# A product that scales w2 moves from POOL to DVE, two tiles change places, and six late sums change engine

## Chip, cores and metric

The kernel runs on one core of one Trainium2 chip. The metric is the time of one execution on the device in microseconds; the kernel before has a median of 1222.18 us over three runs (1219.56 to 1225.83). A core has five engines, each with its own queue of instructions that it works off in order: PE multiplies matrices, DVE, ACT and POOL work elementwise, and SP issues the transfers. They wait for one another through semaphores.

## The reference

A transformer block on 2048 tokens of width D = 576, all in float32, with six vectors of length 576 that are computed from a condition vector `c`:

```python
mod = (_silu(c) @ w_mod).reshape(c.shape[0], 6, 1, -1)
sa, ca, ga, sb, cb, gb = (mod[:, 0], mod[:, 1], mod[:, 2], mod[:, 3], mod[:, 4], mod[:, 5])
h = _layernorm(x, axis=-1) * (1 + ca) + sa
x = x + ga * _A_ref(h, A_wqkv, A_wo)        # linear attention, 32 heads
h = _layernorm(x, axis=-1) * (1 + cb) + sb
x = x + gb * _B_ref(h, B_w1, B_w2)          # silu(h @ w1) @ w2, F = 4608
```

The change concerns the last line, the feed-forward part. Its output is scaled by `gb`, one factor for each output column; the kernel multiplies the columns of w2 by `gb` instead.

## The kernel before

**Three stages.** Up to about 250 us the kernel computes the attention's projections, and up to about 398 us the attention's output, the second layer norm and the first 256 of the 4608 hidden columns. From there to the end it works on the other 17 groups of 256 hidden columns, numbered 1 to 17 (`NG` is 18). This third stage is where the diff lies.

**The third stage.** The tokens are four blocks of 512, taken as two pairs. A unit (class `Unit`) is one group of hidden columns with one pair of blocks. Both multiplications of a unit, up (by w1, `up`, L960) and down (by w2, `down`, L1048), are done in the Strassen-Winograd way: seven products of half-sized matrices in place of eight, for sums and differences of the quarters. Every operand is split into a rounded part, which ACT writes as a cast, and the rest, which DVE or POOL writes as a difference (`sub_hi` at L62, `split` at L1008 and L1009), so that each product takes three passes. The operands of `up` from the tokens have been stored in DRAM (`hd`) and are streamed through three buffers called rooms; each pass that ends starts the next fetch (L936).

**The weights of a group** (class `Weights`). `load1` brings a group's part of w1 into the tile `raw` (L890, and two transfers of 64 rows, L892), `sums1` makes four sums on POOL (L881 to L884) in the temporary tile `t`, and `up(n)` splits operand n into one of eight tiles `w1` (cast L902, difference L62). `load2` brings the group's part of w2 into the same tile `raw` (L908); `sums2` multiplies it by gb (L912, on POOL, 128 partitions of 2 x 576 values), makes four more sums on POOL, and `down` splits the results (cast L924, difference L62). The tile `wt` holds the last 64 rows of w1. `raw`, `t` and the `w1` tiles lie in one pool of SBUF memory, `wm`, with `raw` first; one `raw` exists at a time.

**What a unit computes.** The products of `up` are put together by DVE from PSUM (L977, L984, L998) into tiles `f`, and ACT applies SiLU (L980, L999). `operands1` and `operands2` make the operands of `down`: `ha` and `hb` are split on DVE, `hd`, `hc` and `he` on POOL, which also makes the sums before them (L1018, L1024, L1026, L1029). The products of `down` are added by DVE from PSUM into the output in SBUF, `acc`, or into one tile `U` for each block (L1052).

**U.** One of Winograd's sums is common to three quarters of the output. It is collected in `U` over all groups, and in the last group `add_u` (L1066) adds it to the three quarters of each block, after which the quarters are stored (L1071). For blocks 0, 1 and 3 these sums are on POOL, for block 2 on DVE. Block 3's own last group is computed without Winograd (`plain_operands`, `plain_down`, L1085 to L1089), so its `U` is complete one unit earlier; the program adds it after the last unit's loop.

**Order.** PE's instructions are in the order of the program: in each unit, the seven products of `up` in turn, and between them the fourteen products of `down` of the unit before. The other engines' instructions are ordered by a scheduler that simulates the program, with the program's order as the priority, so an edit in one place can move instructions on DVE, ACT, POOL and SP around it. Two PSUM tiles hold the results of `down`: a product that begins a new sum in one of them waits until DVE has added the old one (L1052), and the second product of a pair in one tile waits until DVE has read the first.

Of the kernel before, what the change touches and what calls it, by code (L numbers as in the profile page):

```python
# [9 lines left out]
F32R = mybir.dt.float32r  # L10
# [5 lines left out]
P = 128  # L16
# [5 lines left out]
def kernel(ctx: ExitStack, tc, A_x, A_wqkv, A_wo, B_x, B_w1, B_w2, c, w_mod, out):  # L22
# [8 lines left out]
    V, A, G, T = nc.vector, nc.scalar, nc.gpsimd, nc.tensor  # L31
# [3 lines left out]
    S, D = x.shape  # L35
# [11 lines left out]
    G2 = 2  # L47
# [13 lines left out]
    def sub_hi(lo, full, hi):  # L61
        return V.tensor_sub(lo, full, f32(hi))  # L62
# [4 lines left out]
    accp = tc.alloc_tile_pool(name="acc", bufs=1)  # L67
    hTa = tc.alloc_tile_pool(name="hTa", bufs=2)
    wg = tc.alloc_tile_pool(name="wg", bufs=2)
    wp = tc.alloc_tile_pool(name="w", bufs=3)  # L70
    wqp = tc.alloc_tile_pool(name="wq", bufs=1, side="right")
# [9 lines left out]
    bc = {n: pool.tile([P, D], F32, name=f"bc_{n}") for n, pool in (("ga", pa), ("gb", const))}  # L81
# [334 lines left out]
    for t in range(NT):  # L416
        tb, i = t // 4, t % 4
# [28 lines left out]
        for _ in range((0, 2, 1, 1)[t] if t < 4 else 1):  # L446
            q = next(qs)
# [42 lines left out]
    for j, kv in enumerate(kvp):  # L490
        n = min(2, NHC - 2 * j)
# [90 lines left out]
    def load_mlp(g):  # L582
        f0 = g * FW
        r1 = rawp.tile([P, KC + 1, FW], F32, name="raw")
        nc.sync.dma_start(r1[:, 0:KC, :], B_w1[0 : KC * P, f0 : f0 + FW].rearrange("(k p) f -> p k f", p=P))
        for h in range(2):
            nc.sync.dma_start(r1[h * 64 : h * 64 + 64, KC, :], B_w1[KC * P : D, f0 : f0 + FW])
        w1 = wg.tile([P, 9, FW], F32R, name="w")
        A.copy(w1[:, 0:KC, :], r1[:, 0:KC, :])
        sub_hi(w1[:, KC : 2 * KC, :], r1[:, 0:KC, :], w1[:, 0:KC, :])  # L590
        wt = rawp.tile([P, 2, FW], F32R, name="wt")
        G.memset(f32(wt[64:128, 1, :]), 0.0)
        tail_w(wt, r1[:, KC, :])
        r2 = rawp.tile([P, KC + 1, FW], F32, name="raw").rearrange("p k f -> p (k f)")[:, : G2 * D]
        r2 = r2.rearrange("p (j d) -> p j d", j=G2)
        nc.sync.dma_start(r2, B_w2[f0 : f0 + FW, :].rearrange("(j p) d -> p j d", p=P))
        w2 = wg.tile([P, G2, 2, D], F32R, name="w")
        V.tensor_mul(r2, r2, bc["gb"].unsqueeze(1).to_broadcast([P, G2, D]))
        A.copy(w2[:, :, 0, :], r2)
        sub_hi(w2[:, :, 1, :], r2, w2[:, :, 0, :])  # L600
        return w1, w2, wt
# [57 lines left out]
    def mlp_units(tb, w):  # L659

        hs = new_hs()
        up = [lambda j=j: mlp_up(tb, w[0], w[2], hs, j) for j in range(G2)]
        return up, [lambda i=i: mlp_down(4 * tb + i, hs, w[1]) for i in range(4)]
# [38 lines left out]
    def turn_all(tb):  # L702
# [16 lines left out]
        else:  # L719
# [29 lines left out]
            else:  # L749
# [3 lines left out]
                for k in CHUNKS:  # L753
                    turn_chunk_k(tb, k, rows[:, k] if k < KC else t)
                    yield
        up, down = mlp_units(tb, w)
        if tb < NB - 1:
            filler.extend(up + down)
# [39 lines left out]
    while s < NT + 5 or filler or turns:  # L798
        if s < QB - 2:
            filler.append(late_q)  # L800
        if s == 4:
            w = load_mlp(0)
# [36 lines left out]
    psC = tc.alloc_tile_pool(name="psC", bufs=1, space=PSUM, reuse_waits="tile")  # L839

    w2p = tc.alloc_tile_pool(name="w2p", bufs=1, reuse_waits="tile")
    wm = tc.alloc_tile_pool(name="wm", bufs=1, reuse_waits="tile")
    pf = tc.alloc_tile_pool(name="pf", bufs=1, reuse_waits="tile")
    first = tc.alloc_tile_pool(name="first", bufs=1, reuse_waits="tile")
    rs = tc.alloc_tile_pool(name="rs", bufs=1, side="right", reuse_waits="tile")
# [4 lines left out]
    U = [pf.tile([P, 2, HALF], F32, name=f"U{b}") for b in range(NB)]  # L850
# [14 lines left out]
    class Weights:  # L865
# [32 lines left out]
            tail_w(self.wt, self.r1[:, KC, :])  # L898

        def up(self, n):  # L900
            w = self.w1[n] = wm.tile([P, 4, P], F32R, name="w1", bufs=8)
            A.copy(w[:, 0:2], self.b1[n])  # L902
            sub_hi(w[:, 2:4], self.b1[n], w[:, 0:2])

# [4 lines left out]

        def sums2(self):  # L910
            r2, t = self.r2, self.temps(HALF)
            G.tensor_mul(r2, r2, bc["gb"].unsqueeze(1).to_broadcast([P, G2, D]))  # L912
            parts = [r2[:, j, k * HALF : (k + 1) * HALF] for j in range(2) for k in range(2)]
            if self.last:
                self.split2("B12", parts[1])
            self.b2 = self.winograd(*parts, [t[:, i] for i in range(3)])
# [14 lines left out]
    def fetch(i):  # L931
        if i < len(streamed):
            _, q, n = streamed[i]
            room = rooms0[ORDER[i]] if i < 3 else rooms[i % 3]
            m = hd[q, n].shape[1]
            nc.sync.dma_start(f32(room[:, :m, :]), hd[q, n])  # L936
            in_room[i] = room

    class Unit:
# [123 lines left out]

        def add_u(self, b, *parts):
            for i, k in parts:
                (V if self.pair == 1 and b == 2 else G).tensor_add(self.c(b, i, k), self.c(b, i, k), U[b])  # L1066

        def store(self, b, i, k):
            t0 = (4 * b + 2 * i) * P
# [21 lines left out]
    with tc.manual_schedule(engines={mybir.EngineType.PE}):  # L1091
        w = Weights(1)
        w.load1()
        w.sums1()
        for n in ORDER:
            w.up(n)
        w.load2()
        for i in range(6):
            fetch(i)
        for u in U:  # L1100
            G.memset(u, 0.0)
        ws = {1: w}
        ph, before = None, None
        units = [(g, p) for g in range(1, NG) for p in range(2)]
        for g, p in units:
            unit = Unit(g, p, ws[g])
            more = g + 1 < NG
            if p == 1 and more:
                ws[g + 1] = Weights(g + 1)
                ws[g + 1].load1()  # L1110
                ws[g + 1].sums1()
            for q, n in enumerate(ORDER):
                if before:
                    before.down(2 * q)
                unit.up(n)
                if before:
                    before.down(2 * q + 1)
                    if q == 0:
                        before.operands1(1)
                        before.operands2(1)  # L1120
                if p == 0 and q == 1:
                    unit.w.sums2()
                if q == 2:
                    if ph is None:
                        first.release()
                        ph = tc.alloc_tile_pool(name="ph", bufs=1, reuse_waits="tile")
                    unit.operands1(0)
                if q == 5:
                    unit.operands2(0)
                if p == 0:  # L1130
                    unit.w.down(*{2: (1, 7), 4: (2, 4), 5: (5, 6), 6: (3,)}.get(q, ()))
                if p == 1 and more:
                    ws[g + 1].up(n)
            if p == 1 and more:
                ws[g + 1].load2()
            before = unit
        unit.plain_operands(1)
        unit.add_u(3, (1, 1), (1, 0), (0, 1))
        for m in range(7):
            unit.down(m)  # L1140
        for t in range(4):
            unit.plain_down(1, t)
    psC.release()
    for p in (rs, ph, pf, wm, w2p, wqp, hTa, accp):
        p.release()


# [26 lines left out]
```

## Time and profile before

| | |
|---|---|
| median of 3 runs | 1222.18 us (1219.56 to 1225.83) |
| the profiled execution | 1227.59 us, its span 1225.9 us |
| PE busy | 1154.5 us (94%) |
| DVE busy | 983.4 us (80%) |
| POOL busy | 654.1 us (53%) |
| ACT busy | 520.7 us (42%) |
| HBM traffic over the span | 218 GB/s |
| POOL, product with gb (L912) | 17 times, 2674 ns each |
| POOL, sums with U (L1066) | 9 times, 1485 ns each |
| DVE, sums with U (L1066) | 3 times, 747 to 750 ns |

A line of a timeline has the start and the duration in us, the engine, the line of the kernel, the operation, the output and input tiles with their shapes, and how many instructions were merged; in brackets stands the idle time of the engine just before and what ended it. A line of the waits has the sum, the number and the longest. A line of windows has a stretch of time, its length and the busy time of each engine in it in the order PE, weight loads, DVE, ACT, POOL, then the granted clock of PE, the share of time in which the DMA engines were busy, and GB/s.

### The profile page before, as it was taken

To read this page: it belongs to the slowest core of one execution; us is meant where nothing else is said; L and a number is where in the kernel's file an instruction comes from. 1 tells how busy PE (TensorE), PEld (TensorE's weight loads), DVE (VectorE), ACT (ScalarE), POOL (GpSimd) and SP (SyncE) were. 2 spreads that over 40 slices of the span, in tenths; PEclk is the share of its full clock that TensorE was granted. 3 is DMA by queue.
4 is the path that set the end of the run, shared out by engine and by line. 5 is a ranking of instruction groups with operands and counts; after the bars stand their busy time and mean duration, and the time that the engine had idled before them with its cause. 6 is when DMAs were issued, how large, how long until landed. Compare 5 with 4: busy or idle time off the path is not lost.

```text
span 1225.9 us, 19275 instructions
## 1 busy us (share of the span) xinstructions
PE 1154.5 (94%) x7167; PEld 1049.2 (86%) x7167; DVE 983.4 (80%) x1551; ACT 520.7 (42%) x1057; POOL 654.1 (53%) x699
## 2 busy tenths in 40 slices
PE   4999999999997899999999999999999999999997
PEld 4999999899987688888888889888888888898896
DVE  6746754888966789888888898888888888888876
ACT  4434242325554444444434444344444444344441
POOL 3200000332501776775776677667757857776784
PEclk9999999999999899999999999999999999999999
DMA  9212300213347777868769668669687687696664
GB/s 278 90 40 88 112 1 1 76 34 126 114 165 292 271 259 278 308 241 322 277 236 339 254 248 331 254 239 331 234 306 287 247 332 265 251 335 258 248 249 144
DMA packets 57579, 268.59 MB, mean 219 GB/s; under 512 B 5450, under 2 KB 20046, under 8 KB 34446
## 3 DMA queue, kind: packets, MB, share of 16 engines
q1 hardware_dynamic: 57486, 267.36, 60.1%
q8 instruction: 57, 0.93, 0.3%
q14 instruction: 36, 0.29, 0.1%
HBM read 250.56 MB, written 16.78 MB: 218 GB/s over the span
## 4 chain that ended last, share of the span: by engine, by line
PE 53%; DVE 22%; POOL 9%; issue 9%; DMA 4%; ACT 3%; SPq 0%; POOLq 0%; ACTq 0%; DVEq 0%
PE up L960 18%; PE down L1048 17%; PE psK L154 9%; DVE w L62 4%; PE big L154 4%; DVE hb L1009 4%; DVE acc L1052 4%; DVE U L1052 3%; DMA raw<-in_B_w_dram 2%; POOL hc L1009 2%; POOL s L1018 2%; DVE f L998 1%; PE big L655 1%; PE small L641 1%; DVE hT L62 1%
## 5 line engine op out<-in xcount | busy, mean ns | idle before, releaser
L1052 DVE TENSOR_TENSOR acc<-down,acc 128x576 f32<-128x576 f32 x335 | 247.4, 747 | 20.7 <-PE down L1048 19.5
L960 PE MATMUL up<-hT,w 128*128 128x512 f32 x876 | 227.9, 395 | 1.3 <-DVE f L998 0.8
L960 PEld LDWEIGHTS up<-hT,w 128*128 128x128 f32 x876 | 156.9, 189 | 27.6 <-DVE f L998 1.2
L1024 POOL TENSOR_TENSOR s<-f,f 128x256 f32<-128x256 f32 x67 | 50.7, 757 | 199.1 <-ACT f L999 158.9
L1048 PE MATMUL down<-w,hc 128*128 128x288 f32 x804 | 123.9, 296 | 13.8 <-DVE acc L1052 13.7
L1052 DVE TENSOR_TENSOR U<-down,U 128x576 f32<-128x576 f32 x134 | 100.1, 747 | 45.0 <-PE down L1048 44.9
L1048 PEld LDWEIGHTS down<-w,hc 128*128 128x128 f32 x804 | 115.3, 188 | 23.4 <-issue 16.2
L1048 PE MATMUL down<-w,hb 128*128 128x288 f32 x804 | 124.6, 297 | 9.1 <-DVE U L1052 7.0
L1048 PEld LDWEIGHTS down<-w,hb 128*128 128x128 f32 x804 | 114.8, 189 | 20.1 <-DVE U L1052 10.5
L154 PE MATMUL psK<-w,hT 128*128 128x288 f32 (+2 forms) x896 | 126.9, 299 | 3.4 <-DVE hT L62 1.3
L154 PEld LDWEIGHTS psK<-w,hT 128*128 128x128 f32 x896 | 122.1, 191 | 5.0 <-DVE hT L62 2.5
L999 ACT ACTIVATE f<-f 128x512 f32<-128x512 f32 x102 | 64.4, 632 | 116.3 <-DVE f L998 116.2
L62 DVE TENSOR_TENSOR w<-raw,w 128x288 fp32r<-128x288 f32 (+2 forms) x139 | 93.5, 682 | 7.9 <-ACT w L902 7.8
L1009 POOL TENSOR_TENSOR hc<-s,hc 128x512 fp32r<-128x512 f32 x67 | 87.9, 1312 | 0.0
L960 PE MATMUL up<-room,w 128*128 128x512 f32 x330 | 84.9, 392 | 1.4 <-DVE f L984 1.4
L1009 DVE TENSOR_TENSOR hb<-f,hb 128x512 fp32r<-128x512 f32 x68 | 83.7, 1231 | 2.1 <-ACT hb L1008 2.1
L62 DVE TENSOR_TENSOR w<-t,w 128x256 fp32r<-128x256 f32 (+1 forms) x102 | 66.7, 654 | 10.1 <-ACT w L902 9.6
L1018 POOL TENSOR_TENSOR s<-f 128x256 f32<-128x256 f32 x67 | 66.0, 985 | 13.4 <-DVE acc L1052 11.2
L1048 PE MATMUL down<-w,hd 128*128 128x288 f32 x402 | 64.9, 297 | 5.9 <-DVE acc L1052 5.9
L1048 PEld LDWEIGHTS down<-w,hd 128*128 128x128 f32 x402 | 57.5, 188 | 14.0 <-ACT f L999 11.9
L1008 ACT CAST hc<-s 128x512 fp32r<-128x512 f32 x67 | 41.5, 620 | 64.0 <-POOL s L1026 64.0
L960 PEld LDWEIGHTS up<-room,w 128*128 128x128 f32 x330 | 58.7, 188 | 11.1 <-DVE f L984 1.8
(228 smaller groups left out, 2401.7 us busy)
## 6 DMA issues: line engine op xcount, KB each, us to landing
hT<-hd SPq DMA_DIRECT2D x69, 1280.0 KB, 5.5
hT<-hd SPq DMA_DIRECT2D x43, 1024.0 KB, 5.3
room<-hd SPq DMA_DIRECT2D x32, 1280.0 KB, 6.3
room<-hd SPq DMA_DIRECT2D x23, 1024.0 KB, 5.0
raw<-in_B_w_dram SPq DMA_DIRECT2D x18, 576.0 KB
raw<-in_B_w_dram SPq DMA_DIRECT2D x18, 512.0 KB, 4.5
hd<-S SPq DMA_DIRECT2D x6, 1024.0 KB
xt<-in_A_x_dram SPq DMA_DIRECT2D x16, 288.0 KB, 5.1
```

The source lines that it names most:

```text
L62: return V.tensor_sub(lo, full, f32(hi))
L154: T.matmul(ps, xpart(a), wpart(b), start=n == 0, stop=n == len(XW) - 1)
L641: T.matmul(ps, left, right, start=n == 0, stop=n == len(seq) - 1)
L655: T.matmul(ps[:, h, :HALF], hs[:, j, a, tok], w2[:, j, b, h * HALF : (h + 1) * HALF], start=n == 0, stop=n == len(seq) - 1)
L960: T.matmul(ps, left, right, start=first and m == 0, stop=m == len(seq) - 1, skip_group_check=True)
L999: A.activation(f, f, AF.Silu)
L1008: A.copy(t[:, :, 0, :], src)
L1009: eng.tensor_sub(t[:, :, 1, :], src, f32(t[:, :, 0, :]))
L1018: G.tensor_sub(s3, half(i, 0, 0), half(i, 0, 1))
L1024: G.tensor_add(s[:, 0:1], half(i, 0, 1), half(i, 1, 1))
L1048: T.matmul(ps[:, p, :HALF], self.a[i, n][:, u, p * P : (p + 1) * P], self.w.w2[n][:, v], start=n in (1, 5, 7, 6) and j == 0, stop=j == 2, ...
L1052: V.tensor_add(dst, ps[:, :, :HALF], dst)
```

## The change

Three edits, all in the third stage. First, the product of w2 with gb is computed by DVE, one instruction for each of the two halves of 128 x 576, in place of one POOL instruction. Second, the eight `w1` tiles get a pool of their own, `w1p`, allocated before `wm`: they lie where `raw` and `t` lay before, and `raw` and `t` lie behind them. Third, the sums with U are on DVE for blocks 0, 1 and 2 and on POOL for block 3 only, and block 3's are written in the middle of the last unit (behind its fourth product of `up`) instead of after it.

```diff
     w2p = tc.alloc_tile_pool(name="w2p", bufs=1, reuse_waits="tile")
+    w1p = tc.alloc_tile_pool(name="w1p", bufs=1, reuse_waits="tile")
     wm = tc.alloc_tile_pool(name="wm", bufs=1, reuse_waits="tile")
...
         def up(self, n):
-            w = self.w1[n] = wm.tile([P, 4, P], F32R, name="w1", bufs=8)
+            w = self.w1[n] = w1p.tile([P, 4, P], F32R, name="w1", bufs=8)
             A.copy(w[:, 0:2], self.b1[n])
...
         def sums2(self):
             r2, t = self.r2, self.temps(HALF)
-            G.tensor_mul(r2, r2, bc["gb"].unsqueeze(1).to_broadcast([P, G2, D]))
+            for j in range(G2):
+                V.tensor_mul(r2[:, j], r2[:, j], bc["gb"])
...
         def add_u(self, b, *parts):
             for i, k in parts:
-                (V if self.pair == 1 and b == 2 else G).tensor_add(self.c(b, i, k), self.c(b, i, k), U[b])
+                (G if b == 3 else V).tensor_add(self.c(b, i, k), self.c(b, i, k), U[b])
...
                         before.operands2(1)
+                if unit.last and p == 1 and q == 3:
+                    unit.add_u(3, (1, 1), (1, 0), (0, 1))
                 if p == 0 and q == 1:
                     unit.w.sums2()
...
         unit.plain_operands(1)
-        unit.add_u(3, (1, 1), (1, 0), (0, 1))
         for m in range(7):
```

In the built program PE's order is the same. On DVE the two products stand between the sum into U and the split of `hb` where that split stood before, and some splits of w and sums around them change places; on POOL `hc` moves up by some places. Block 3's sums with U stand at almost the same place of POOL's order as before.

More of the change, by code (lines that the diff above doesn't have):

```diff
@@ L1143 @@
     psC.release()
-    for p in (rs, ph, pf, wm, w2p, wqp, hTa, accp):
+    for p in (rs, ph, pf, wm, w1p, w2p, wqp, hTa, accp):
         p.release()
```

## The prediction

> **What bounds it now.** I read the page's busy line first, then windows of one weight group each (two units) in the long second half, then PE's waits there, then the timelines of one such window on three engines side by side.
>
> ```profile
> PE 1154.5 (94%) x7167; PEld 1049.2 (86%) x7167; DVE 983.4 (80%) x1551; ACT 520.7 (42%) x1057; POOL 654.1 (53%) x699
> ```
> ```profile
> 630.69:678.39 47.70, 46.00 (x269) 40.82 (x268) 41.37 (x63) 20.98 (x45) 33.63 (x38) 1.00 0.75 280
> ...
> sum 715.43, PE 691.15 PEld 613.63 DVE 618.50 ACT 314.69 POOL 507.83; mean PE 46.08 PEld 40.91 DVE 41.23 ACT 20.98 POOL 33.86
> ```
> ```profile
> PE down L1048 <- DVE acc L1052: 19.1, 30, 0.9
> PE down L1048 <- DVE U L1052: 4.7, 11, 1.2
> PE up L960 <- DVE f L984: 0.5, 1, 0.5
> ```
> A window takes 47.70 us, PE works 46.00 of it at full clock, and over 15 windows (715.43 us) PE's idle is 24.3 us, all of it waiting for DVE. So the kernel is PE-bound, and what a change can win here is these waits. Where they come from, DVE, POOL and PE at one place:
>
> ```profile
> 630.02 0.75 DVE L1052 TENSOR_TENSOR U<-down,U 128x576 f32<-128x576 f32 x1
> 630.69 3.08 DVE L1009 TENSOR_TENSOR hb<-f,hb 128x512 fp32r<-128x512 f32 x1
> 633.70 0.68 DVE L998 TENSOR_TENSOR f<-up,p 128x512 f32<-128x512 f32 x1
> 634.30 0.74 DVE L1052 TENSOR_TENSOR acc<-down,acc 128x576 f32<-128x576 f32 x1
> ...
> 637.71 1.57 DVE L62 TENSOR_TENSOR w<-t,w 128x288 fp32r<-128x288 f32 x1
> 639.21 1.41 DVE L1052 TENSOR_TENSOR acc<-down,acc 128x576 f32<-128x576 f32 x2
> ```
> ```profile
> 629.85 0.74 POOL L1024 TENSOR_TENSOR s<-f,f 128x256 f32<-128x256 f32 x1 [6.18 <-ACT f L999]
> 630.55 2.68 POOL L912 TENSOR_TENSOR raw<-raw,bc_gb 128x1152 f32<-128x1152 f32 x1
> ...
> 637.68 1.29 POOL L1009 TENSOR_TENSOR hc<-s,hc 128x512 fp32r<-128x512 f32 x1
> ```
> ```profile
> 635.18 1.02 PE L1048 MATMUL down<-w,hd 128*128 128x288 f32 x6 [0.38 <-DVE acc L1052]
> ...
> 640.10 1.04 PE L1048 MATMUL down<-w,hc 128*128 128x288 f32 x6 [0.93 <-DVE acc L1052]
> ```
> The split hb takes 0.67 when POOL is idle (at 627.48). Here it begins 0.14 after POOL's product with gb and ends 0.54 after it: 3.08, so 2.4 lost. The split of w at 637.71 loses 1.1 (0.45 alone) in the same way behind POOL's hc. DVE's sums that read PSUM are 0.74 to 0.76 throughout. So a DVE instruction with both inputs in SBUF and a POOL instruction exclude each other, and the two PE stalls, 0.38 and 0.93, are DVE running late after that block. The pair stands in every window: 30 waits, 19.1 us.
>
> **The product moves to DVE.** In what follows a window is the 47.7 us from 630.69 to 678.39. Gone from POOL: 17 times 2.68. New on DVE: 17 pairs of 128x576. The nearest rows are the three DVE sums of L1066 (750 ns each, 2.08 for three, so 0.67 apart) and the single 128x1152 product of L598, 1.286. I take 0.67+0.74 = 1.41 a pair; by the single one it would be 1.29. The Trainium skill ("Perfetto Trace Analysis", Optimizing Scalar/DVE Operations) speaks for grouping on a busy engine, with about 60 ns of overhead per DVE instruction on SBUF: by it the second part costs an estimated 17 x 0.06 = 1.0 us, by the rows 17 x 0.12 = 2.0.
>
> In the built order the pair stands between U and hb, where hb stood blocked. Queued behind it are hb, f, acc, w, U, ha, w, acc, acc; PE waits for the first and the last but one of these sums. Times by the rows: U ends 630.69; POOL's next sum (0.70, from 630.55) may hold the first product to 631.25; product, product and hb follow without a gap, and at 668.3 three such DVE instructions ran on while a POOL one waited, so 0.67+0.67+0.60 gives 633.2; f 0.60 and acc 0.67 give 634.5, against 635.04 now. PE is free at 634.80: the first stall is gone. Then w 0.37, U 0.67, ha 0.33, w 0.37, acc 0.67, acc 0.67 and one more POOL block, 0.8, give 638.4. PE would be there at 640.10-0.93-0.38-0.1 = 638.7: the second stall goes too, narrowly. I take 1.1 of 1.31, plus 0.15 because the first group after a stall runs 1.02 to 1.04 instead of 0.95: 1.25 x 15 = 18.8 us. Bounds: 1.31+0.39+0.3 = 2.0 a window if the third stall (U, 0.39 at 672.39, behind a POOL sum of 1.70 that DVE held up) goes too; a loss of 0.7 a window if hc, which moves up into this stretch, gets in before hb (1.25) and two more POOL instructions of 0.75 elsewhere.
>
> The pair waits for the load of w2 (L908), which POOL took before. It is issued at 626.29 and L912 started 4.26 later, directly behind L1024, in nearly every window, so it had landed. DVE comes to it 4.4 after the issue: no wait.
>
> In the middle of the window the built order puts f of L984 in front of a U, and that f waits for POOL's he of the unit before (647.76 to 648.49 now). Behind it are U and, at 649.23, PE's hb. POOL has 2.68 less to do ahead of that he, which covers the earlier place; 0, and up to +0.5 a window if POOL is late.
>
> First group: the load lands at 407.3 and L912 then holds ha for 2.85. Now DVE itself waits to 407.3, then 1.41+0.41, so it is 1.0 earlier; but two more w splits stand before U, for which PE waits 2.30 there: +0.75. I take 0, between -1.1 and +1.5.
>
> **Places of w1 and raw.** The queue SP has the same transfers in the same order up to the first raw load, which waits for the same transfer as before; what holds it is two stores of S on the queue ahead and its 11.1 us in flight. Cost 0. Later the two 64-row tails of raw are issued together instead of around a room load; the room load comes up to 1.0 (two issues of 0.5) later, and PE showed no wait for a room in the 15 windows. The split of wt moves ahead of f; DVE's 1.48 idle at 666.05 waiting for it covers it, and if the tails were late, f and two sums would be behind that. 0, between -0.4 and +0.4 a window.
>
> **Sums with U.** Block 3's three stay on POOL and land between the same neighbours (1180.9 to 1187.7); 0. Six others leave POOL for DVE, 0.67 apart.
>
> ```profile
> 1192.74 2.83 POOL L1066 TENSOR_TENSOR acc<-acc,U 128x576 f32<-128x576 f32 x2
> 1195.52 1.31 POOL L1009 TENSOR_TENSOR hc<-s,hc 128x512 fp32r<-128x512 f32 x1
> 1196.77 0.77 POOL L1009 TENSOR_TENSOR hd<-s,hd 128x256 fp32r<-128x256 f32 x1
> 1197.47 1.43 POOL L1066 TENSOR_TENSOR acc<-acc,U 128x576 f32<-128x576 f32 x1
> 1198.82 0.75 POOL L1009 TENSOR_TENSOR he<-f,he 128x256 fp32r<-128x256 f32 x1
> ```
> ```profile
> 1200.35 1.65 PE L960 MATMUL up<-S,w 128*128 128x512 f32 x6 [2.65 <-DVE f L984]
> ```
> POOL has no gap here, and f (1199.61) waits for this he. Without 2.83+1.43 he ends near 1195.3; f follows by 1196.5, PE is free at 1197.7: 2.65 saved. The three sums take 2.0 of DVE's 3.67 idle between 1193 and 1200. The other three (block 1) held hc to 1.66 instead of 0.67, and PE 1.63 at 1211.28; now they cost DVE 2.0 in a stretch with 2.6 idle. I take half, 0.8. The stores, in order on SP, now wait for DVE instead of POOL; the last four start after 1218.6 either way. Tail: -3.4, between -4.5 (both stalls and the 0.21 between them) and +1 (2.0 more on DVE, 1.0 of block less, no idle used).
>
> **Sum.** -18.8-3.4 = -22.2 against the profiled 1227.59 (span 1225.9 and 1.7 around it): 1205.4. That execution lies 5.4 above the median 1222.18, so I forecast 1200 for the median.
>
> **Rivals.** (a) All three stalls go: 15 x 2.0+3.4+1 = 34, 1188. For it: POOL's chain before the third stall loses one DVE block. Against: the 1.70 hangs on how the two engines interleave. 0.10.
>
> (b) The block only changes places: hc, now right behind the product, and the short POOL sums hold the DVE pair and hb as long as L912 did, 2.4 less 1.41 being eaten up. For it: w at 637.71 lost 1.1 to hc. Against: DVE ran on without a gap at 668.3. Only the tail is won: 1219 (1214 to 1223). 0.18. The Trainium skill (same page and section) says that moving work between DVE and POOL might not help because they share a read port; that is this case, and the trace so far agrees on the exclusion (3.08 against 0.67), not on the size.
>
> (c) Slower: the product on DVE waits for the load of w2, in order, with everything behind it. By the sum above, a landing at 6.3 (the room loads' median) still leaves 1.1 of stall in place of 1.31; it costs from about 6.5 us on, one for one. At 7.8, which a raw load took once (at 798.94), it is +1.3 a window: 1222+19-3 = 1238. Against: 4.26 was always enough, and DMA share is 0.75. 0.10.
>
> That the change does nothing holds for two of its parts, the places and block 3, and is in the sum.
>
> **Numbers.** Forecast 0.62 (1193 to 1209). 0.5%, about what a measurement can tell from no change, is 6.1 us: faster is below 1216. Faster: 0.62+0.10+0.06 of (b) = 0.78; same: 0.12 of (b) and 0.02 of a mild (c), 0.14; slower 0.08. The range 1188 to 1219 leaves out (c), half of (b) and little of (a), 0.2.
>
> **What shows it.** Right: hb's mean falls from 1231 to about 750 ns; PE's waits for acc in the middle fall from 19.1 to a few us; a window near 46.4; the product at about 0.75; PE's 2.65 before up<-S gone. Wrong: the products at over 1.2 each or idle in front of them for the load; hb still above 1000; PE's waits for acc or U as large as before; a new wait of f L984 for POOL's he in front of U.

## Result and the profile after

The changed kernel takes 1219.01 us (median of 20 runs, 1214.46 to 1224.16) against 1224.45 us of the kernel before in the same batch: ratio 0.9956, interval 0.9939 to 0.9974, a gain of 5.4 us where 22 were forecast. The profiled execution took 1217.73 us, its span 1215.7.

The medians of the kernel before lay between 1222 and 1229 us in the batches told of here, so kernels are compared by their ratio to it in their own batch. One source of scatter is the part up to the first product of `down`, in which the kernels differ in little but the first group's product with gb: that product of `down` began anywhere between 410.5 and 419.6 us in the 13 profiled executions. That is why stages are compared below, each by itself.

The page's busy line (as before, less POOL, more DVE instructions):

```profile
PE 1158.4 (95%) x7167; PEld 1048.1 (86%) x7167; DVE 984.3 (81%) x1591; ACT 518.2 (43%) x1057; POOL 599.8 (49%) x676
```

Next, the fifteen windows from the second group's first product of `down` to the last group's, as one stretch, and the tail behind them up to the end of the span:

```profile
463.03:1171.64 708.61, 693.43 (x4023) 611.32 (x4021) 616.08 (x947) 311.14 (x677) 464.04 (x541) 1.00 0.78 283
1171.64:1215.73 44.09, 36.31 (x226) 32.41 (x224) 35.11 (x47) 9.84 (x19) 20.40 (x20) 1.00 0.40 145
```

The same two stretches in the kernel before:

```profile
466.63:1181.00 714.37, 690.00 (x4023) 612.40 (x4022) 618.18 (x917) 313.32 (x677) 506.75 (x556) 1.00 0.76 280
1181.00:1225.85 44.85, 36.39 (x226) 32.54 (x224) 29.98 (x41) 10.15 (x19) 27.65 (x26) 1.00 0.39 141
```

A window is 708.61/15 = 47.24 us; by the same two marks it was 714.37/15 = 47.62 before. The forecast had about 46.4. The tail is 44.09 against 44.85. PE's waits in these fifteen windows:

```profile
PE down L1050 <- DVE U L1054: 11.9, 25, 1.5
PE down L1050 <- DVE acc L1054: 2.2, 3, 1.0
```

Before, by the same marks, it was 19.6 for acc and 4.7 for U. The waits for acc that the prediction wanted gone are gone but for 2.2, and waits for U stand in their place. Two DVE groups of the page's kind, by line (busy time, mean ns of one, idle in front):

```profile
L1011 DVE TENSOR_TENSOR hb<-f,hb 128x512 fp32r<-128x512 f32 x68 | 49.6, 729 | 0.1
L914 DVE TENSOR_TENSOR raw<-raw,bc_gb 128x576 f32<-128x576 f32 x34 | 33.4, 1023 | 3.2 <-DMA raw<-in_B_w_dram 3.2
```

The split `hb` is free (1231 ns before). The place itself, DVE, then POOL, then PE, in one window:

```profile
1098.34 1.97 DVE L914 TENSOR_TENSOR raw<-raw,bc_gb 128x576 f32<-128x576 f32 x2
1100.22 0.68 DVE L1011 TENSOR_TENSOR hb<-f,hb 128x512 fp32r<-128x512 f32 x1
...
1101.43 0.74 DVE L1054 TENSOR_TENSOR acc<-down,acc 128x576 f32<-128x576 f32 x1
1102.09 1.05 DVE L62 TENSOR_TENSOR w<-raw,w 128x288 fp32r<-128x288 f32 x1
1103.07 0.75 DVE L1054 TENSOR_TENSOR U<-down,U 128x576 f32<-128x576 f32 x1
```
```profile
1102.02 0.81 POOL L882 TENSOR_TENSOR t<-raw 128x288 f32<-128x288 f32 x1
```
```profile
1103.96 1.03 PE L1050 MATMUL down<-w,hb 128*128 128x288 f32 x6 [0.62 <-DVE U L1054]
```

A split of the new w (L62) stands between the sum into acc and the sum into U. In the kernel before, U came directly behind acc (at 634.96) and the split behind it. Here the split, 0.45 us when POOL is quiet, is held by POOL's sum `t` and takes 0.98 up to the start of U; so U is late, and PE, which needs it before its product with `hb`, waits 0.62. Thirteen of the fifteen windows show this wait (0.60 to 0.63 in twelve, 1.50 in one). In the other two, POOL's `hc` gets in between the two products and `hb` (at 815.87 and 958.10), `hb` takes 1.77, and PE waits 0.99 for acc instead.

### The profile page after: what moved, and what is told of

Read it like the earlier page. It is cut to its first block, busy times and chain, and to the rows that moved or that the text cites. A ratio compares the mean times of both kernels' runs of the same rounds, so it can differ in the third digit from the quotient of the medians.

```text
span 1215.7 us, 19355 instructions
## 1 busy us (share of the span) xinstructions
PE 1158.4 (95%) x7167; PEld 1048.1 (86%) x7167; DVE 984.3 (81%) x1591; ACT 518.2 (43%) x1057; POOL 599.8 (49%) x676
## 5 line engine op out<-in xcount | busy, mean ns | idle before, releaser
L1054 DVE TENSOR_TENSOR acc<-down,acc 128x576 f32<-128x576 f32 x335 | 245.7, 748 | 22.2 <-PE down L1050 17.1
L1050 PE MATMUL down<-w,hb 128*128 128x288 f32 x804 | 127.2, 300 | 15.0 <-DVE U L1054 13.6
L1054 DVE TENSOR_TENSOR U<-down,U 128x576 f32<-128x576 f32 x134 | 100.7, 752 | 48.6 <-PE down L1050 47.6
L1011 POOL TENSOR_TENSOR hc<-s,hc 128x512 fp32r<-128x512 f32 x67 | 94.4, 1409 | 12.0 <-ACT hc L1010 12.0
L62 DVE TENSOR_TENSOR w<-raw,w 128x288 fp32r<-128x288 f32 (+2 forms) x139 | 83.3, 609 | 7.4 <-ACT w L903 7.0
L154 PE MATMUL big<-w,qT 128*128 128x288 f32 x448 | 65.8, 300 | 0.8 <-DVE qT L62 0.7
L1028 POOL TENSOR_TENSOR s<-s,f 128x256 f32<-128x256 f32 x67 | 64.6, 964 | 2.7
L962 PE MATMUL up<-hT,wt 128*128 128x512 f32 x206 | 64.9, 396 | 0.0
```

Source lines behind the costliest of these rows:

```text
L154: T.matmul(ps, xpart(a), wpart(b), start=n == 0, stop=n == len(XW) - 1)
L962: T.matmul(ps, left, right, start=first and m == 0, stop=m == len(seq) - 1, skip_group_check=True)
L1011: eng.tensor_sub(t[:, :, 1, :], src, f32(t[:, :, 0, :]))
L1028: G.tensor_sub(s[:, 1:2], s[:, 0:1], half(i, 0, 0))
L1050: T.matmul(ps[:, p, :HALF], self.a[i, n][:, u, p * P : (p + 1) * P], self.w.w2[n][:, v], start=n in (1, 5, 7, 6) and j == 0, stop=j == 2, ...
L1054: V.tensor_add(dst, ps[:, :, :HALF], dst)
```

## Experiments

Window: the fifteen windows' stretch divided by 15. Tail: from the last group's first product of `down` to the end of the span, which comes about 1.2 us after the last store's data. (The expectations count the tail to the last computing instruction, 3.0 us less, or 4.3 to 4.4 less in the three kernels with moved sums.) Both come from one profiled execution each; the ratio comes from all runs against the kernel before.

| kernel | median us | ratio and interval | window | tail |
|---|---|---|---|---|
| before | 1222.21 to 1228.85 | 1 | 47.62 | 44.85 |
| changed | 1219.01 | 0.9956 (0.9939 to 0.9974) | 47.24 | 44.09 |
| changed, again | 1217.03 | 0.9947 (0.9919 to 0.9975) | 47.15 | 44.95 |
| before + product alone | 1218.29 | 0.9933 (0.9905 to 0.9960) | 47.16 | 43.33 |
| changed, product on POOL | 1223.36 | 0.9973 (0.9947 to 0.9999) | 47.45 | 45.21 |
| changed + one edge | 1208.22 | 0.9846 (0.9817 to 0.9875) | 46.43 | 43.98 |
| the same, again | 1209.19 | 0.9862 (0.9822 to 0.9902) | 46.60 | 45.10 |
| one edge, no product | 1206.79 | 0.9848 (0.9818 to 0.9879) | 46.42 | 44.13 |
| three edges | 1200.74 | 0.9816 (0.9783 to 0.9848) | 46.13 | 44.77 |
| changed + moved sums | 1216.17 | 0.9941 (0.9919 to 0.9964) | 47.15 | 42.00 |
| one edge + moved sums | 1205.25 | 0.9834 (0.9799 to 0.9870) | 46.42 | 42.12 |
| three edges + moved sums | 1201.82 | 0.9819 (0.9785 to 0.9853) | 46.18 | 42.06 |
| one edge, six sums left out | 1203.62 | 0.9823 (0.9790 to 0.9857) | 46.58 | 40.76 |

The theory (A) after the result: the product's move works as forecast, but in the new order a split of w stands in front of the sum into U, loses to POOL there and makes PE wait. The rival (B): DVE and POOL hinder each other for a fixed sum of work, and a stall taken away comes back at another place.

**The parts by themselves.** The product alone, with pool and sums as before:

```diff
-            G.tensor_mul(r2, r2, bc["gb"].unsqueeze(1).to_broadcast([P, G2, D]))
+            for j in range(G2):
+                V.tensor_mul(r2[:, j], r2[:, j], bc["gb"])
```

> The kernel before with only the product of w2 with gb moved to DVE in two parts; the pool of w1 and the sums with U stay as they were. Theory A (the gain of the changed kernel is the product's alone, in the fifteen middle windows): within 2 us of the changed kernel, 1217 to 1221. Rival B (the new places of w1 and raw take part of the gain away, or give it): the time lies more than 3 us from the changed kernel, and the windows of the trace (47.2 us each there) differ by over 0.2 us. Rival C (the moved sums with U bring something after all): 3 us or more slower than the changed kernel, with all of it behind 1148 us.

It came out like the changed kernel: windows of 47.16, 1218.29 us, a ratio of 0.9933 that can't be told from 0.9956. The rest without the product, which is the changed kernel with that diff turned round:

> The changed kernel with the product back on POOL in one instruction: what is left of the change is the pool of w1 and the sums with U on DVE. Theory A: nothing is left, 1222 to 1227, windows of 47.7 us, hb again at a mean of about 1.2 us. Rival B (places matter): more than 3 us off the kernel before in either direction, with windows that differ by over 0.2 us. Rival C (the sums matter): 3 us or more faster than before, all of it behind 1148 us.

PE's waits in its fifteen windows are those of the kernel before:

```profile
PE down L1049 <- DVE acc L1053: 16.7, 25, 1.0
PE down L1049 <- DVE U L1053: 4.6, 12, 0.4
```

So the windows' gain is the product's, as theory A has it. The ratio 0.9973 leaves room for a small gain of the rest: 3.3 us, barely outside its interval. The profile gives it no clear place (0.17 us a window, a tail 0.4 longer), and the two parts together (0.9933 and 0.9973) make more than the whole (0.9956); the intervals are too wide to say whether that is real.

**The split of w behind U.** One order edge: the split of w2's operands 1 and 7 is issued on DVE only behind the earlier unit's first sum into U.

```diff
-                    unit.w.down(*{2: (1, 7), 4: (2, 4), 5: (5, 6), 6: (3,)}.get(q, ()))
+                    with behind([before.added[0]] if before and q == 2 else []):
+                        unit.w.down(*{2: (1, 7), 4: (2, 4), 5: (5, 6), 6: (3,)}.get(q, ()))
```

(`added[m]` keeps the instruction of L1054 for product m.)

> The changed kernel with one order edge more: the split of w2's operands 1 and 7 may be issued on DVE only behind the sum of the earlier unit's product into U that PE waits for before hb. Theory A (the split of w in front of that sum takes 0.4 to 1.05 us and makes U late by 0.6 us in twelve windows): PE's waits for U lose about 0.5 us a window, windows of 46.6 to 46.8 instead of 47.2, some 7 to 9 us in all: 1210 to 1212. Rival B (DVE and POOL hinder each other for a fixed sum of work, and a stall that goes in one place comes back in another): PE's waits for acc or ha, hc behind the split grow by what those for U lose; windows within 0.15 us of 47.2, time within 2 us of the changed kernel. Rival C: the split, held back, comes too late for PE's weight loads of w: slower than the changed kernel by 3 us or more, with waits of PE for w.

Theory A, and by more than it asked: windows of 46.43, 1208.22 us. The same place in its timeline, PE's waits in the fifteen windows, and the stretch:

```profile
1088.44 0.74 DVE L1054 TENSOR_TENSOR acc<-down,acc 128x576 f32<-128x576 f32 x1
1089.11 0.74 DVE L1054 TENSOR_TENSOR U<-down,U 128x576 f32<-128x576 f32 x1
1089.77 0.44 DVE L62 TENSOR_TENSOR w<-raw,w 128x288 fp32r<-128x288 f32 x1
```
```profile
PE down L1050 <- DVE U L1054: 4.6, 15, 0.6
PE down L1050 <- DVE acc L1054: 2.6, 14, 0.2
```
```profile
461.13:1157.56 696.43, 689.22 (x4023) 610.61 (x4021) 610.20 (x947) 311.36 (x677) 466.21 (x541) 1.00 0.78 288
```

No work was added or removed. U runs beside POOL's work, the split comes after it and takes 0.44 instead of 1.05, and 7.3 us of waits for U are gone while those for acc grow by 0.4. The stretch is shorter by 12.2 us (708.61 to 696.43). The listed waits make up 7.2 of it, gaps too short to be listed 0.8, and PE's busy time 4.2 (693.43 to 689.22). That last part is mostly at the same place: at the wait in the changed kernel the last matmul in front counts with its whole 0.30 us, where the next one otherwise begins after 0.13, and the first one behind counts 0.21 in place of 0.13. Rival B, that the stall only changes places, falls. A second batch gave 0.9862 and a window of 46.60 (two windows of 47.6 among others of 46.4):

> The kernel with the one order edge again, beside the two variants of its end in this batch, since the part ahead of the windows, where all kernels are alike, took anything from 410 to 420 us in the profiled runs, as much as the end can bring: ratio to the kernel before 0.982 to 0.988, tail from the last group's first product 41 to 42 us.

**The price of the product.** The kernel with the edge, the two products left out:

> The kernel with the order edge, with the product of w2 with gb left out altogether (the factor gb is missing from the output). It prices the product where it now stands on DVE. Theory A (with the product in front of hb and f, hb ends 1.4 to 2 us later than it could, but PE comes to it still later, so that it is hidden): within 3 us of the kernel with the order edge. Rival B (the product's 1.4 to 2.0 us on DVE are still paid in the windows): faster than the kernel with the order edge by 0.5 us or more a window, 8 us or more in all.

Windows 46.42 against 46.43, ratio 0.9848 against 0.9846: at this place the product on DVE costs nothing that can be measured. The forecast's "hidden" was right, and the missing gain was not the product's own time.

**Two more edges.** The split of operand 7 goes behind the third product's sum, and one split of w1 goes behind the eighth's sum into U.

```diff
-                    unit.w.down(*{2: (1, 7), 4: (2, 4), 5: (5, 6), 6: (3,)}.get(q, ()))
+                    for p2 in {2: (1, 7), 4: (2, 4), 5: (5, 6), 6: (3,)}.get(q, ()):
+                        with behind([before.added[p2 // 3]] if before and q == 2 else []):
+                            unit.w.down(p2)
...
-                    ws[g + 1].up(n)
+                    with behind([before.added[7]] if q == 3 else []):
+                        ws[g + 1].up(n)
```

> The kernel with the order edge and two more: the split of w2's operand 7 only behind the sum of the third product of the earlier unit, and one split of w1 only behind the sum into U of the eighth. Theory A (what is left in a window are two waits for DVE's sums, 0.42 us for U and 0.33 us for acc, each from a split issued in front of them): both lose most, windows of 45.8 to 46.1 us instead of 46.4, time 1198 to 1203 on a chip where the kernel with one edge takes 1208. Rival B (DVE as a whole is late; holding a split back only moves the wait): windows within 0.15 us of 46.4. Rival C (the held split of w1 makes PE wait for w1, or the next group's up): slower by 3 us or more with waits for w.

The waits fall again:

```profile
PE down L1050 <- DVE acc L1054: 2.1, 3, 1.0
PE down L1050 <- DVE U L1054: 1.9, 7, 0.6
```

The windows, 46.13 in the mean, end a little above the expected 45.8 to 46.1: most take about 45.6 or 46.2, the first and the last 46.9 and 47.2, and a wait for U comes back seven times. 1200.74 us, ratio 0.9816.

**The tail.** In the changed kernel, DVE and POOL at the first three of the moved sums, and PE's two larger waits behind them:

```profile
1182.96 4.30 DVE L1068 TENSOR_TENSOR acc<-acc,U 128x576 f32<-128x576 f32 x3
```
```profile
1184.18 1.25 POOL L1011 TENSOR_TENSOR hd<-s,hd 128x256 fp32r<-128x256 f32 x1
1185.40 1.25 POOL L1011 TENSOR_TENSOR he<-f,he 128x256 fp32r<-128x256 f32 x1
```
```profile
1187.99 1.84 PE L1050 MATMUL down<-w,hb 128*128 128x288 f32 x12 [1.24 <-DVE U L1054]
1198.55 1.06 PE L1050 MATMUL down<-w,hd 128*128 128x288 f32 x6 [1.84 <-DVE acc L1054]
```

The sums take turns with `hc`, `hd` and `he` on POOL, one for one: 4.30 us instead of 2.08 (what three of them take at the very end, with POOL idle), and `hd` 1.25 instead of 0.74. The next sums into U and acc are queued behind them.

In the kernel with the product alone, where these sums are still on POOL, PE's waits in the tail are 2.12, 0.60 and 0.29 us, 3.0 in all against 3.8 here, and its tail is 43.33 against 44.09: by these two profiles the tail's gain over the kernel before is the product's, and the moved sums gave part of it back.

Three kernels put block 0's sums on POOL behind that `he`, where POOL idles for 6.9 us, and block 1's on DVE between the plain sums of the end, where DVE waits for PE (`s` below is the plain sum of tile 1 for two of them, of tile 2 for the third):

```diff
-                (G if b == 3 else V).tensor_add(self.c(b, i, k), self.c(b, i, k), U[b])
+                (G if b in (0, 3) else V).tensor_add(self.c(b, i, k), self.c(b, i, k), U[b])
...
+                        with behind([he]):
+                            before.add_u(0, (1, 1), (1, 0), (0, 1))
...
+                with behind([s]):
+                    first_of_last.add_u(1, (i, k))
```

> The changed kernel once more, on the same chip as the runs of this batch, so that they can be set against it: ratio to the kernel before 0.994 to 0.997 by every theory.

> The changed kernel with its six sums of blocks 0 and 1 with U elsewhere: block 0's on POOL behind the split of he, where POOL idles for 6.9 us; block 1's on DVE behind the second and third plain sum of the end. Theory A (those six sums on DVE, alternating with hc, hd and he on POOL, make U and acc late: 1.3, 2.0 and 0.9 us of waits of PE): the three waits go, 3 to 4 us less than the changed kernel, all behind its last group's start. Rival B (POOL's sums now hinder DVE's U, acc and f sums by as much, or the end is set by the plain sums): within 1 us of the changed kernel, with waits of PE of the same sum at other places. Rival C: block 1's late sums put the last store off: up to 1 us slower.

> The three edges and the moved sums of the end together. Theory A: the gains add, 3 to 4 us below the kernel with three edges, 1195 to 1200 on a chip where the kernel before takes 1225. Rival B: the sums on POOL bring nothing, the time is that of the three edges within 1 us.

The tails are 42.00 and 42.06 against 44.95 and 44.77 of the kernels without the move: 2.7 to 3.0 us less, near the 3 to 4 of theory A. Yet the medians lie 0.9 below and 1.1 above theirs, which theory A did not expect. A third batch was run for this, with a kernel that leaves the six sums out:

> The kernel with the one order edge and the moved sums of the end (block 0's on POOL behind he, block 1's on DVE behind plain sums). Theory A (the 4 us by which the traces of the two kernels with these sums moved are shorter at the end are real; their medians did not show them because the part ahead of the windows scatters): the tail is 37.5 to 38 us again and the median 3 to 5 us below the kernel with the one edge. Rival B (what the end gives is taken back somewhere else in each run, by later stores or a longer head): median within 1.5 us of the kernel with the one edge.

> The kernel with the one order edge without the six sums of blocks 0 and 1 with U (these blocks of the output lack U's part). It prices the six sums. Theory A: the same tail as with the sums moved, within 1 us (they are hidden there), 37 to 38 us, and 3 to 5 us below the kernel with the one edge. Rival B (the waits at the end come from hc, hd and he on POOL against DVE's other sums, not from the six): tail above 39.5 us.

```profile
1174.10 4.21 POOL L1070 TENSOR_TENSOR acc<-acc,U 128x576 f32<-128x576 f32 x3
```
```profile
1160.14:1202.26 42.12, 36.07 (x226) 32.53 (x224) 31.15 (x44) 9.76 (x19) 22.79 (x23) 0.99 0.42 151
```

These are lines of the kernel with one edge and moved sums: POOL does block 0's three in its gap. Its last computing instruction ends 37.74 us into the tail, as without the six sums (37.74 in both), so up to there the six sums cost nothing. The end still comes later, 42.12 against 40.76: from the last computing instruction to the end it is 4.4 us with the moved sums and 3.0 without. Block 1's quarters wait for their late sums, so three more stores fall among the four of the plain sums: SP issues seven from 1193.6 on instead of four. Rival C of the first of these kernels expected such a delay, of up to 1 us; that the late stores are its cause was not tested by itself.

Part of the scatter of the tails is the clock. In four of them ("changed, again", "changed, product on POOL", "the same, again", "three edges") the granted clock was 0.96 and PE was busy 37.4 to 37.8 us, in all others 36.1 to 36.5. Without those four, the tail is 43.98 to 44.13 us with the six sums as the change has them, 42.00 to 42.12 with the sums moved, and 40.76 without them. So the six sums cost the tail 3.2 to 3.4 us as the change places them, and 1.2 to 1.4 when moved.

In the third batch the medians follow, 1205.25 and 1203.62 against 1209.19. Whether all of the gain reaches the median stays open: the three pairs give -0.9, +1.1 and -3.9 us, and the part ahead of the groups alone scatters by 9.

The lowest ratio is that of the kernel with three edges, 0.9816. Its version with moved sums, 0.9819, can't be told from it.

## Why the prediction was wrong, by its own steps

- **The pair's own time and place: right.** In the first group, where POOL is quiet, it took 1.43 (forecast 1.41). In most windows it takes 1.97, because POOL's short sum (L1028) gets in once. The forecast had 0.56 for such a hold, and `hb` ends 2.5 us after U ends, as forecast. Leaving the product out gains nothing.
- **First and second stall, 0.38 and 0.93: right.** `hb` is at 729 ns (forecast 750), and the waits for acc fell from 19.6 to 2.2 us over fifteen windows.
- **The failed step is the list of what is queued behind `hb`, priced with "Then w 0.37, U 0.67" and read with "PE waits for the first and the last but one of these sums".** Two things are wrong in it. The U in that list is awaited as well, by PE's first product with `hb`, and it was left out. And the w in front of it was priced at 0.37, the duration without POOL beside it; it took 0.98. The difference, 0.61, is the wait: 0.62. The step did have "one more POOL block, 0.8", but as one lump at the end of the list, where it counts for the last sums only and not for U. The built order showed the split in front of U, and the trace of before had its price (the w at 637.71, held by `hc`, and the one at 636.06, 1.06). With that order mended, the windows fall by 1.19 us (47.62 to 46.43) and by 1.02 in the second batch; the forecast was 1.25. Without its tail the forecast is 1203.4, and the kernel with one edge, at 0.9846 and 0.9862 of 1222.18, is 1203.4 and 1205.3.
- **The tail, -3.4: mis-sized.** Measured -0.8, and +0.1 in the second profile, where the granted clock was 0.96. PE's wait of 2.65 before up<-S is gone, as forecast. But "the three sums take 2.0 of DVE's 3.67 idle" was wrong: they were issued as soon as their inputs were there, in front of the next U, beside `hc`, `hd` and `he`, which had moved up because POOL was free. That gave 1.24, 1.84 and 0.75 of new waits in place of 2.65, 1.63 and 0.21. The bounds (-4.5 to +1) held.
- **Costs at nothing: right as far as the runs show.** The load of w2 holds DVE in the first group (3.02 of the 3.2 us in the line above) and in one window (0.18), no wait of PE for f shows in the fifteen windows, and with the places of w1 and raw changed the windows are 47.24 and 47.15, with the product alone 47.16. The ratios of these kernels can't be told apart, so a few us in all, either way, are not excluded.
- **The rivals.** (c), the load, came as 0.18 us of one window. (b) gave 1219, which is the time measured, but that is luck: it let POOL's `hc` take the place of the product in front of `hb`, which happened in two windows of fifteen, while in the others `hb` is free; and it won the tail, where almost nothing was won. Its heading, that the block only changes places, is nearest to the truth: the block came back in one split of w behind `hb`, and PE felt it only because of that split's place. (a), all stalls gone, 1188, is not reached by three edges either: 0.9816 of 1222.18 is 1200.

The Trainium skill says of moving work between DVE and POOL that it might not help, because the two share a read port ("Perfetto Trace Analysis", Optimizing Scalar/DVE Operations). The runs here bear that out only in part: as it was made, the move gained 0.4%, and with one order edge more the changed kernel is 1.4 to 1.5% below the kernel before.

## What to carry to other kernels

When a move frees an engine, list again every instruction of the new order for which the critical engine waits, and price what stands in front of each one with its duration beside the other engine's work, not alone. Where two engines exclude each other on some instructions only, put those that are not touched (here the sums from PSUM, which PE waits for) first, and let the touched ones, which nobody needs soon, come after; an order edge did this here without any new work. An instruction with slack, like these six sums, should be held back explicitly where a scheduler issues it as soon as it can, but with an eye on the stores that wait for it: here the end behind the last computing instruction grew from 3.0 to 4.4 us.

## What the runs showed of the hardware

DVE's sums of `down`, which read PSUM, keep 0.74 to 0.76 us whatever POOL does, while the split of w with two inputs in SBUF takes 0.44 in one run and 1.05 in the other at the same place, by what POOL has begun just before. The Trainium skill states this ("SBUF — State Buffer", Who interferes with whom): a DVE instruction with two SBUF inputs contends with a POOL instruction that reads SBUF, one with at most one such input (outside the modes that use two ports) does not, and the shared pair of ports is an exclusive lock. The traces agree in these durations, and the experiment with one edge makes use of it.

Not expected was how a run of such DVE instructions fares. In thirteen of the fifteen windows the two products and `hb` let one POOL sum in and then ran without a gap. At the end three sums in a row alternated with three POOL splits, each waiting for one of the other engine: 4.30 us against 2.08. A difference between the two places is that POOL had its next instruction ready each time at the end, while in the windows its `hc` was still waiting for ACT's cast (0.73 us idle in front of it). In the other two windows POOL's sum was through ahead of the second product (0.73 us, where it otherwise takes 1.37), `hc` was ready before `hb`, and it did get in. That fits, but whether it decides was not tried.
